# Packed attention with a gated convolution: lower parts of the weights summed on TensorE, some subtractions on VectorE, 1e-9 as a 33rd column

## The chip, the cores and the metric

The kernel runs on one core of one Trainium2 chip, in one launch. The metric is device time in microseconds (us). Before the change three runs took 299.49, 299.0 and 297.74 us: median 299.0 us. Engines: PE is TensorE (PEld its weight loads), DVE is VectorE, ACT is ScalarE, POOL is GpSimd, SP issues all transfers.

## The reference

Eight batches of eight heads, 576 positions, 64 columns per head. A packed set of 32 queries `p` attends over the sequence; the 576 queries `q` then attend over those 32 results; a gated convolution block follows. `w_val`, `conv_w` and `w_out` arrive as 64-bit numbers, all else as 32-bit.

```python
def sm_attn(qq, kk, vv):
    s = scale * np.matmul(qq, kk.transpose(0, 1, 3, 2))
    s = s - np.max(s, axis=-1, keepdims=True)
    a = np.exp(s)
    a = a / (np.sum(a, axis=-1, keepdims=True) + 1e-09)
    return np.matmul(a, vv)
p_packed = sm_attn(p, k, v)
out = sm_attn(q, p_packed, p_packed)
...
for k in range(K):
    gate_pre += conv_w[k][None, None, :] * xp[:, k:k + S, :]
gate = 1.0 / (1.0 + np.exp(-gate_pre))
val = x @ w_val
return (gate * val @ w_out).astype(np.float32)
```

## The kernel before

Every batch is cut into steps, each a Python generator that yields after an instruction or a few. A table, `ORDER`, spells out the sequence in which the steps are advanced; a letter is a step, the digit behind it the batch, and `.n` means n advances. `InOrder` ties each instruction to the one before it on its engine, so the table fixes each engine's queue, and an instruction that waits holds up all that stand behind it there. Between engines only data and buffers make anything wait. The helper has one line (L82), so the profile's rows are told apart by the names of their tiles.

The steps: `P K V Q` load p, k, v, q; `L` loads the weights as pairs of 32-bit words; `W`, `C`, `O` turn `w_val`, `conv_w`, `w_out` into 32-bit form; `k` and `q` transpose on DVE; `a` is the first attention (scores `s<-kT`, the maximum `nb`, the exponential `a<-s`, a transpose `at`/`a1t` on PE and ACT, the product `pv` with v, the normalised `ppd`); `p` turns `ppd` into `ppT`; `s` makes the second scores (`s<-qT`), transposes them on DVE into `t`, takes the maximum `mx`, subtracts on POOL, exponentiates on ACT; `t` sums (`sm`), inverts (`rs`), scales on POOL, transposes back (`a<-t`), and splits the result into a rounded part `a2h` and a remainder `a2l`; `w` multiplies `ppT` by `w_val` (`wp`, split into `wph` and `wpl`); `x` makes the attention output `x` for the gate, in batches 0 to 2 already convolved (`kx`, from `cwb`) and in batches 3 to 7 copied to `xp`; `g` is the gate of batches 3 to 7, four chained multiply-adds per 128 channels on DVE (`sig<-xp,cw,sig`) and a tanh on ACT; `v` multiplies gate and value (`val` on PE, `sig<-sig,val` on DVE) and splits that into `gvh` (a copy on ACT) and `gvl` (a subtraction on POOL); `o` is the projection, twelve matmuls for each 128 output rows from `gvh`, `gvl`, `woh`, `wol`, then a copy `osb` out of PSUM and a store.

`from_double` builds a number from its two words: `top`, from the high word, and `rest`, the low word scaled on ACT, then multiplied on POOL by the power of two of `top`. For `w_val` POOL adds the two (`wv`). For `w_out` ACT rounds half of `top` to `woh`, DVE takes the remainder, and POOL adds `rest` to it (`wol`). The half stands for the 1/2 in sigmoid(z) = (1 + tanh(z/2))/2. The tiles of the weights lie in a pool `stage`, whose space is taken over by `gvh` and `gvl` afterwards; there are two `top` buffers and five of `words`. PSUM has three buffers of two banks (`big`) and two of one bank (`mid`, `out`).

Of the kernel before, what the change touches and what calls it, by code (L numbers as in the profile page):

```python
# [47 lines left out]
ORDER = """
L0 W0 P0 L0 P0 W0.2 k0 K0 W0 k0 K0 W0 L0 W0 V0 K1 W0 k0 a0 W0.2 a0.4 W0 a0.3 W0.3 K1 k1 W0 a0 k1 a0 L0 Q0 W0 k1 L0
a0.2 W0 V0 W0.2 a0 Q0 L0 W0 C0 q0 a1 C0 a1 C0 a0 W0 a1 a0 a1 V1 W0 K2 a1 C0.2 a0 a1 a0 q0 p0.2 O0 C0 a1 s0 C0 O0 a1 s0  # L50
O0 P2 a1 s0.2 L0 s0 O0 s0 O0.2 a1 Q1 a1.2 C0 t0.2 C0 V1 O0.2 C0 s0 W0.3 t0 P2 t0 s0.2 O0 t0 k2 a1 k2 t0.2 W0 C0 O0.2
x0 q1 t0 W0 a1 W0 O0 W0 a1 x0 Q1 a1 w0 O0 a1 q1 O0 t0 O0 p1 O0.2 L0 x0 K2 x0 K3 w0 O0.2 k2 O0 w0 O0 x0 L0 O0 x0 t0
O0.4 a2 O0 x0 v0 O0 k3 V2 p1 O0 a2.2 K3 a2 O0.2 v0 O0 a2 O0 V2 s1 O0.2 s1 a2 O0 | s1 a2.2 s1 v0 a2.2 v0 a2 v0 s1.2 x1
a2 k3 v0.2 t1 v0 t1 v0 s1 a2 w1 a2 w1 P4 a2 v0.2 K4 k3 Q2 t1 s1 v0 a2 w1 a2 v0 P4 p2 t1 V3 v0 s1 v0 t1 a3 t1 V3 v0 t1
a3.2 k4 p2 a3 t1 a3 Q2 t1 a3 o0 a3 x1 k4 a3 q2 t1 a3 x1 o0 x1 q2 a3 x1.2 v1 x1 K4 k4 s2 v1 a3 v1 s2.2 v1 a3 Q3 s2.2 o0
v1 s2 Q3 v1 s2 o0 a3 v1 a4 x2 q3 t2 a3 a4 o0 a4 a3 s2 a3 v1.2 o0 K5 k5 a3 t2 v1 a4.2 s2 t2.2 o0 Q4 a4 p3 t2 P6 o0.2 v1
q3 t2 v1 p3 v1 Q4 v1 a4.2 w2 t2 w2 s3 k5 t2 s3 v1.2 w2 t2 s3.2 t2 V4 s3 o0 K5 o0 x2.2 V4 s3 w3 q4 a4 x2.2 t3 s3 q4 t3
k5 x3 K6 s3 w3 a4 t3 w3 o1 t3.2 a4 s3 t3 x2.2 o1 V5 o1 v2 a4 v2 t3.2 P6 a5 a4 a5 t3 o1 a5 K6 a5.2 v2.2 a4 x3.2 o0 k6
a4 x3 t3 a4.2 x3 a5.2 x3 g3 k6 a5 p4.2 x3 v2 a5 V5 a5.2 k6 a5 g3.2 v2 g3 v2.2 s4 g3 v2 s4.2 o1 g3.2 o1 s4 o1 Q5 g3
s4.2 g3 v2 a5 g3 s4 a5 v2.2 g3 v2 t4 a5 o1 g3 a6 s4 v2 a5 o1.2 t4 g3 q5 o1 a6 g3 t4 w4 Q5 v2 a5 a6 g3 a6 o1 w4 K7 o1  # L60
q5 v2 t4 g3 p5 w4 g3 a6 p5 s4 v3 V6 s5 v3 t4 o1 k7 Q6 t4 v3.2 g3.3 v3 s5 v3 V6 o2 t4 g3 o2 s5 v3 s5 o2 g3 v3.2 t4.2 s5
o2 v3 s5 g3 x4 o1 t4 Q6 v3 o2 v3 x4 o2 x4 v3 x4.2 s5 g3 t5 o2 x4 k7 g4 v3 g4 a6 s5 g4 v3 t5 x4 a6 o2 a6 w5 a6 t5.2 a6
o2 g4 a6 g4 q6 g4 a6 g4 a6 g4 t5 v4 g4 a6 s5 o2.2 a6 g4 w5 t5 g4.2 w5 v4 v3 g4 a6 g4 o3 a6 t5 v4.3 g4 o3 p6 t5 v4.2 p6
v4 g4 o2 v4 g4.3 Q7 q6 v4 o3 g4.4 x5.3 K7 o3 s6 o3.2 v4 V7 t5 o3 s6 x5 v4 x5 o3 k7 s6.2 t5 x5 o3 g5 o3 s6.2 Q7 g5.2 x5
o3 a7 g5 g4 a7 v5 g5 a7 o3 g5 V7 s6 g5 a7.2 o3 v5 s6 a7 g5 v4 a7 o3 s6 v5 a7 o3 t6 w6 a7 v5 w6 g5 v4.2 g5 a7.3 v4 g5
q7 a7 g5 v5 o4 q7 a7 g5 a7 g5 v5 o4 t6 a7 o4 v5 o4 v5 g5 t6 g5 w6 g5 t6.2 a7 p7 o4 t6.2 v5 p7 g5 o4 s7 g5 o4 g5 s7 t6
s7.2 o4 v5 s7.2 o4 g5.3 x6 t6 s7 x6 s7 v5.2 t6 x6 o4 x6.2 v5 o4 g5 t7 v5 x6 g6.3 v5 g6 s7 g6 v5 x6 g6 v6.2 o5 t7 o4 t7
o5 g6 w7 g6 o5.2 t7 g6 o5 t7 g6.2 v6.2 g6 t7 v6 g6 v6 g6.2 o5.2 g6 o5 w7 v6.2 g6 v6 g6 o5.2 w7 g6 v6 g6 t7 g6.3 o5 v6
o5 x7 t7 v6.2 g6 v6 o5 x7 o5 t7 v6.2 o6 x7 o5 x7.2 t7 v7 o6.2 x7 g7.2 o6 g7.3 o6 g7 v7 g7 v7 g7 x7 v7.2 o6 g7 o6.2
g7.3 v7 g7 o6 g7.2 v7.3 g7 o6.2 g7.2 v7 g7 o7 g7 o7 v7.2 g7 v7 g7 o7 g7.2 v7.2 o7 v7 o7.2 o6 o7.13  # L70
# [28 lines left out]
def packed_attention_gated_conv(  # L99
# [329 lines left out]
    def attn_out(b):  # L429
        t2 = st["t2", b] = tile_of("t2", [P, G, NBLK, NP], F32, f"t2_{b}")  # L430
        mx = tile_of("mx2", [P, G, NBLK], F32, f"mx2_{b}")
        s2s = scores(
# [3 lines left out]
        for g in range(G):  # L436
            dve.transpose(
                t2[:, g].rearrange("a y z -> a (y z)").rearrange("a (c i m) -> a c i m", c=2, i=NP),
                in_turn(s2s[g]),
            )  # L440
            yield
            for gs in parts(b):
                if gs.stop != g + 1:
                    continue
                n = gs.stop - gs.start
                t3 = t2[:, gs].rearrange("a g y z -> a (g y) z")
                m3 = mx[:, gs].rearrange("a g y -> a (g y)")
                dve.tensor_reduce(m3, t3, axis=AX.X, op=ALU.max)
                yield
                pool.tensor_tensor(  # L450
                    t3, t3, m3.unsqueeze(2).broadcast_to([P, n * NBLK, NP]), op=ALU.subtract
                )
                yield
                act.activation(t3, t3, AF.Exp, scale=scale)
                yield

    def weighted(b):
        sm = tile_of("sm2", [P, G, NBLK], F32, f"sm2_{b}")
# [4 lines left out]
        for gs in parts(b):  # L463
            n = gs.stop - gs.start
            t3 = st["t2", b][:, gs].rearrange("a g y z -> a (g y) z")
            s3, r3 = (x[:, gs].rearrange("a g y -> a (g y)") for x in (sm, rs))
# [11 lines left out]
            yield
            act.copy(ah[:, gs], a2[:, gs])
            yield  # L480
            (pool if b < 3 else dve).tensor_tensor(al[:, gs], a2[:, gs], ah[:, gs].bitcast(F32), op=ALU.subtract)
# [248 lines left out]
```

## Time and profile before

| | |
|---|---|
| three runs, median | 299.0 us |
| the profiled execution, its own time | 301.0 us |
| its span, first to last instruction | 299.2 us |
| mean granted TensorE clock | 0.945 |
| PE busy | 259.6 us (87%), 3676 matmuls |
| DVE busy | 245.2 us (82%), 349 instructions |
| ACT busy | 164.4 us (55%) |
| POOL busy | 124.6 us (42%) |
| read from HBM, written | 33.57 MB, 9.44 MB |

A row of a grouped view reads: line, engine, operation, output<-input, partitions x elements, count | busy us, mean ns of one | idle time of the engine just before, and what ended it. A row of the timeline or of the chain reads: start, duration, engine, operation, and in brackets the idle time before it and its releaser. In the table by stretches each engine has its busy us, and the last three columns are the granted TensorE clock (1.00 is full speed), the DMA engines' busy share and GB/s.

### The profile page before, as it was taken

How to read it: one execution, taken by the hardware profiler on the slowest of the kernel's cores; microseconds unless marked ns; L12 is line 12 of the kernel's file. 1: busy time of each engine (PE TensorE's matmuls, PEld its weight loads, DVE VectorE, ACT ScalarE, POOL GpSimd, SP SyncE). 2: the span in 40 equal slices, each digit the busy share in tenths (PEclk: the TensorE clock that was granted, in tenths of full speed). 3: DMA queues.
4: the chain of work that ended last, by engine and by line, in shares of the span. 5: the costliest groups of instructions: out<-in, count | busy, mean ns of one | idle time of the engine just before them, and what ended most of it. 6: DMA issues, size and time to landing. Idle time of an engine off the chain costs nothing.

```text
span 299.2 us, 8542 instructions
## 1 busy us (share of the span) xinstructions
PE 259.6 (87%) x3676; PEld 192.0 (64%) x3676; DVE 245.2 (82%) x349; ACT 164.4 (55%) x306; POOL 124.6 (42%) x107
## 2 busy tenths in 40 slices
PE   0465555989999998999999999999999979999984
PEld 0143343457677874768776768867876758778852
DVE  1499569799977898687999999999999989847841
ACT  4155345576753564477573766657764637546412
POOL 1334358659916474314424741541522803511230
PEclk9998555899999999999999999999999979999998
DMA  7999996534952498355467511565010101111004
GB/s 219 303 334 265 271 278 200 149 84 157 290 160 70 142 298 226 95 144 156 139 169 196 184 37 46 184 163 183 37 71 37 38 35 70 62 45 70 35 2 175
DMA packets 25839, 43.56 MB, mean 146 GB/s; under 512 B 5829, under 2 KB 11973, under 8 KB 25802
## 3 DMA queue, kind: packets, MB, share of 16 engines
q1 hardware_dynamic: 25802, 43.02, 48.6%
q8 instruction: 29, 0.48, 0.7%
q14 instruction: 8, 0.07, 0.1%
HBM read 33.57 MB, written 9.44 MB: 144 GB/s over the span
## 4 chain that ended last, share of the span: by engine, by line
PE 56%; DVE 23%; DMA 9%; ACT 5%; issue 3%; SPq 2%; POOL 1%; POOLq 1%; ACTq 0%; DVEq 0%
PE o L82 23%; DVE sig L82 13%; PE val L82 11%; PE x L82 8%; PE s L82 5%; DMA vm<-in_v_dram 3%; PE pv L82 3%; DMA wo_words<-in_moe_w_out_dram 3%; PE at L82 3%; DMA km<-in_k_dram 2%; DVE sm L82 2%; DVE kT L82 2%; SPq L82 2%; PE wp L82 1%; ACT sig L82 1%
## 5 line engine op out<-in xcount | busy, mean ns | idle before, releaser
L82 DVE SCALAR_TENSOR_TENSOR sig<-xp,cw,sig 128x576 f32<-128x576 f32 x80 | 76.5, 957 | 8.7 <-ACT sig L82 7.2
L82 POOL TENSOR_TENSOR gvl<-sig,gvh 128x576 fp32r<-128x576 f32 x32 | 48.4, 1514 | 79.7 <-ACT gvh L82 79.7
L82 PE MATMUL o<-woh,gvh 128*128 128x512 f32 x144 | 59.0, 410 | 2.8 <-ACT osb L82 2.7
L82 PE MATMUL o<-woh,gvl 128*128 128x512 f32 x144 | 57.3, 398 | 1.0 <-POOL gvl L82 1.0
L82 PE MATMUL o<-wol,gvh 128*128 128x512 f32 x144 | 56.9, 395 | 0.0
L82 PE MATMUL val<-a2h,wph 128*128 128x288 f32 x128 | 39.6, 310 | 0.0
L82 PE MATMUL val<-a2h,wpl 128*128 128x288 f32 x128 | 37.8, 295 | 0.0
L82 PE MATMUL val<-a2l,wph 128*128 128x288 f32 x128 | 37.7, 294 | 0.0
L82 ACT COPY osb<-o 128x512 f32<-128x512 f32 x34 | 19.9, 587 | 31.4 <-PE o L82 25.2
L82 PEld LDWEIGHTS o<-woh,gvh 128*128 128x128 f32 x144 | 27.4, 190 | 15.0 <-ACT osb L82 6.3
L82 PEld LDWEIGHTS o<-woh,gvl 128*128 128x128 f32 x144 | 27.3, 190 | 8.3 <-POOL gvl L82 2.1
L82 DVE SCALAR_TENSOR_TENSOR sig<-sig,val 128x576 f32<-128x576 f32 x32 | 23.7, 740 | 9.9 <-PE val L82 5.6
L82 PEld LDWEIGHTS o<-wol,gvh 128*128 128x128 f32 x144 | 27.5, 191 | 4.8
L82 POOL TENSOR_TENSOR t<-t,mx 128x576 f32<-128x576 f32 x16 | 20.8, 1299 | 19.5 <-DVE mx L82 19.4
L82 PE MATMUL pv<-vm,a1t 96*32 96x64 f32 x768 | 16.7, 239 | 13.9 <-ACT a1t L82 8.0
L82 POOL TENSOR_TENSOR t<-t,rs 128x576 f32<-128x576 f32 x16 | 20.6, 1288 | 17.7 <-DVE rs L82 15.0
L82 PEld LDWEIGHTS pv<-vm,a1t 96*32 96x32 f32 x768 | 13.4, 121 | 22.5 <-ACT a1t L82 14.4
L82 PE MATMUL s<-kT,pT 32*32 32x288 f32 x512 | 17.2, 479 | 12.1 <-DVE kT L82 11.7
L82 ACT CAST gvh<-sig 128x576 fp32r<-128x576 f32 x32 | 21.5, 673 | 10.5 <-DVE sig L82 9.4
L82 PEld LDWEIGHTS val<-a2h,wph 128*128 128x128 f32 x128 | 24.1, 188 | 5.0 <-DVE sig L82 1.4
L82 PEld LDWEIGHTS val<-a2h,wpl 128*128 128x128 f32 x128 | 24.1, 188 | 0.4
L82 PEld LDWEIGHTS val<-a2l,wph 128*128 128x128 f32 x128 | 24.1, 188 | 0.0
(81 smaller groups left out, 457.7 us busy)
## 6 DMA issues: line engine op xcount, KB each, us to landing
km<-in_k_dram SPq DMA_DIRECT2D x16, 576.0 KB, 6.1
vm<-in_v_dram SPq DMA_DIRECT2D x16, 576.0 KB, 7.1
qm<-in_q_dram SPq DMA_DIRECT2D x16, 576.0 KB, 5.3
out_dram<-osb SPq DMA_DIRECT2D x36, 256.0 KB, 2.1
wv_words<-in_moe_w_val_dram SPq DMA_DIRECT2D x4, 512.0 KB, 5.9
wo_words<-in_moe_w_out_dram SPq DMA_DIRECT2D x4, 512.0 KB, 10.2
p<-in_p_dram SPq DMA_DIRECT2D x16, 64.0 KB, 3.5
cw_words<-in_moe_conv_w_dram SPq DMA_DIRECT2D x1, 20.0 KB
```

What stands on the lines that cost most here:

```text
L82: made = getattr(self.engine, op)(*args, **kw)
```

## The change

1. `rest` gets a tile of its own (two buffers) in place of the low words. Two constants, `plus` and `minus`, are the identity times 1 and -1. `wv` is now summed by two matmuls (`top` under the identity, `rest` under `plus`) into the `out` bank of PSUM and copied out by ACT. `woh` is `top` rounded, without the half; its remainder is summed by three matmuls (`top`, minus `woh`, plus `rest`) and copied out by ACT. The half is applied where `osb` leaves PSUM.
2. `gvl` of batches 3 to 7 is subtracted on DVE; in batches 0 to 2 on POOL as before.
3. `t` has rows of 33 words; POOL writes 1e-9 into the last of each, and the sum `rs` runs over 33. The addition of `eps` goes. The sums of the first attention get one tile for both halves, so 1e-9 and the reciprocal are one instruction each per batch.
4. The order table is another one. A branch for joined halves (`parts`, not used at `JOINED = 8`) is gone.

```diff
-L0 W0 P0 L0 P0 W0.2 k0 K0 W0 k0 K0 W0 L0 W0 V0 K1 W0 k0 a0 W0.2 a0.4 W0 a0.3 W0.3 K1 k1 W0 a0 k1 a0 L0 Q0 W0 k1 L0
+L0 W0 P0.2 W0.2 K0 W0 L0 K0 W0.2 k0 W0.3 V0 Q0 W0 k0.2 a0 W0 k1 K1 a0 W0.2 a0.2 K1 q0 L0 W0 a0.3 W0 a0 k1 a0 W0.2 L0
...
+    nc.scalar.mul(plus, ident, 1.0)
+    nc.scalar.mul(minus, ident, -1.0)
-    eps = const.tile([P, G * NBLK], F32, name="eps")
-    nc.gpsimd.memset(eps, 1e-9)
...
-            pool.tensor_tensor(rest, rest, hw.bitcast(F32), op=ALU.mult)
...
+        pool.tensor_tensor(rest, low, hw.bitcast(F32), op=ALU.mult)
...
-            pool.tensor_tensor(
-                wv[:, c, :], st["top", f"wv{c}"], words[:, :, 0].bitcast(F32), op=ALU.add
-            )
+            whole = one(f"wv{c}_ps", "out")
+            pe.matmul(whole, ident, st["top", f"wv{c}"], start=True, stop=False)
+            pe.matmul(whole, plus, st["rest", f"wv{c}"], start=False, stop=True)
+            yield
+            act.copy(wv[:, c, :], whole)
...
-            act.mul(hi, top, 0.5)
-            yield
-            dve.scalar_tensor_tensor(
-                top, top, 0.5, hi.bitcast(F32), op0=ALU.mult, op1=ALU.subtract
-            )
-            yield
-            pool.tensor_tensor(lo, top, rest, op=ALU.add)
+            act.copy(hi, top)
+            yield
+            left = one(f"wo{c}_ps", "out")
+            pe.matmul(left, ident, top, start=True, stop=False)
+            pe.matmul(left, minus, hi, start=False, stop=False)
+            pe.matmul(left, plus, rest, start=False, stop=True)
+            yield
+            act.copy(lo, left)
...
-            dve.tensor_scalar_add(rs, rs, 1e-9)
-            dve.reciprocal(rs, rs)
+        dve.tensor_scalar_add(sm, sm, 1e-9)
+        dve.reciprocal(sm, sm)
...
-        t2 = st["t2", b] = tile_of("t2", [P, G, NBLK, NP], F32, f"t2_{b}")
+        t2 = st["t2", b] = tile_of("t2", [P, G, NBLK, NP + 1], F32, f"t2_{b}")
+        pool.memset(t2[:, :, :, NP:], 1e-9)
...
-            dve.tensor_reduce(s3, t3, axis=AX.X, op=ALU.add)
-            dve.tensor_tensor(s3, s3, eps[:, : n * NBLK], op=ALU.add)
-            dve.reciprocal(r3, s3)
+            dve.tensor_reduce(r3, t3, axis=AX.X, op=ALU.add)
+            dve.reciprocal(r3, r3)
...
-            pool.tensor_tensor(
+            (pool if b in ON_POOL["gvl"] else dve).tensor_tensor(
                 lo, gv, hi.bitcast(F32), op=ALU.subtract
             )
...
-                dve.tensor_copy(osb, ops)
+                dve.tensor_scalar(osb, ops, 0.5, None, op0=ALU.mult)
             else:
-                act.copy(osb, ops)
+                act.mul(osb, ops, 0.5)
```

PE's queue ahead of the first convolution (`x_0_0`, `x_0_1` of batch 0), before. `at_1` and `pv_1` belong to the second half of batch 1's first attention, `cwps` and `spread` to the convolution's weights:

```order
L82 MATMUL pv_0_412<-vm_0_326,a1t_0_352 32x64 x24
L82 MATMUL cwps<-ident,cw_top 128x5 x4
L82 MATMUL spread<-cw_top,ident 32x64 x40
L82 MATMUL at_1_527<-ident,a_1_1_331 96x64 x12
L82 MATMUL pv_1_561<-vm_1_467,a1t_1_526 32x64 x24
L82 MATMUL x_0_0_590<-a_0_459,kx_551 64x288 x2
```

The same place after the change:

```order
L83 MATMUL pv_0_423<-vm_0_361,a1t_0_343 32x64 x24
L83 MATMUL at_1_465<-ident,a_1_1_336 96x64 x12
L83 MATMUL cwps<-ident,cw_top 128x5 x4
L83 MATMUL spread<-cw_top,ident 32x64 x40
L83 MATMUL wo_ps<-wo_top,ident 128x512
L83 MATMUL wo_ps<-woh,minus 128x512
L83 MATMUL wo_ps<-wo_rest,plus 128x512
L83 MATMUL pv_1_556<-vm_1_363,a1t_1_464 32x64 x24
L83 MATMUL ppTt_598<-ident,ppd_342 128x128 x3
L83 MATMUL wv_ps<-wv_top,ident 128x512
L83 MATMUL wv_ps<-wv_rest,plus 128x512
L83 MATMUL x_0_0_609<-a_0_484,kx_550 64x288 x2
```

A sum for `w_out` and the last one for `w_val` have come in ahead of the convolution, with batch 1's `ppTt`. Of the other three sums for `w_val` the first is PE's first work, the second stands within batch 0's first attention, the third right ahead of its second scores; the other three for `w_out` come behind the convolution's first half.

DVE's queue in the second softmax of batch 0 (`t`, `mx`, `sm`/`rs`, `a`), before, from the transposition of the second half:

```order
L82 STREAM_TRANSPOSE t_0_366<-s_0_1_369 128x576
L82 TENSOR_SCALAR wo_words<-wo_top 128x512
L82 TENSOR_SCALAR sm_1_1_332<-sm_1_1_332 128x1
L82 RECIPROCAL sm_1_1_332<-sm_1_1_332 128x1
L82 TENSOR_REDUCE sm_0_457<-t_0_366 128x18
L82 TENSOR_TENSOR sm_0_457<-sm_0_457,eps 128x18
L82 RECIPROCAL rs_0_458<-sm_0_457 128x18
L82 COPY cw<-cwps 128x20
L82 SCALAR_TENSOR_TENSOR wo_top<-wo_top,woh 128x512
L82 TENSOR_REDUCE mx_0_367<-t_0_366 128x18
L82 TENSOR_SCALAR wv_words<-wv_words 128x512
L82 STREAM_TRANSPOSE a_0_459<-t_0_366 128x576
```

The same place after:

```order
L83 STREAM_TRANSPOSE t_0_383<-s_0_1_387 128x18x32
L83 TENSOR_REDUCE mx_0_384<-t_0_383 128x18
L83 SCALAR_TENSOR_TENSOR wo_top<-wo_top,wo_words 128x512
L83 TENSOR_REDUCE rs_0_483<-t_0_383 128x18
L83 RECIPROCAL rs_0_483<-rs_0_483 128x18
L83 COPY cw<-cwps 128x20
L83 TENSOR_SCALAR wo_words<-wo_top 128x512
L83 STREAM_TRANSPOSE a_0_484<-t_0_383 128x576
L83 TENSOR_SCALAR wv_words<-wv_words 128x512
L83 TENSOR_REDUCE rs_0_483<-t_0_383 128x18
L83 RECIPROCAL rs_0_483<-rs_0_483 128x18
```

The second maximum now stands right behind its transposition, and the work on `wv_words` behind the first `a<-t`.

DVE's queue at the end, the last two quarters of batch 7's gate and value, before:

```order
L82 SCALAR_TENSOR_TENSOR sig_2_3668<-xp_1_3514,cw,sig_2_3668 128x576 x4
L82 SCALAR_TENSOR_TENSOR sig_2_3668<-sig_2_3668,val_2_3675 128x576
L82 SCALAR_TENSOR_TENSOR sig_3_3707<-xp_1_3514,cw,sig_3_3707 128x576 x4
L82 SCALAR_TENSOR_TENSOR sig_3_3707<-sig_3_3707,val_3_3741 128x576
L82 COPY osb_5_3791<-o_4_3709 128x512
```

And after:

```order
L83 SCALAR_TENSOR_TENSOR sig_2_3661<-xp_1_3494,cw,sig_2_3661 128x576 x4
L83 TENSOR_TENSOR gvl<-sig_1_3608,gvh 128x576
L83 SCALAR_TENSOR_TENSOR sig_2_3661<-sig_2_3661,val_2_3672 128x576
L83 SCALAR_TENSOR_TENSOR sig_3_3686<-xp_1_3494,cw,sig_3_3686 128x576 x3
L83 TENSOR_TENSOR gvl<-sig_2_3661,gvh 128x576
L83 SCALAR_TENSOR_TENSOR sig_3_3686<-xp_1_3494,cw,sig_3_3686 128x576
L83 SCALAR_TENSOR_TENSOR sig_3_3686<-sig_3_3686,val_3_3738 128x576
L83 TENSOR_TENSOR gvl<-sig_3_3686,gvh 128x576
```

The subtraction `gvl` of a quarter stands behind gate work of the next one; on POOL the same rows are gone, and only the softmax's subtractions and scalings are left there for these batches.

More of the change, by code (lines that the diff above doesn't have):

```diff
@@ L32 @@
  'qm': 2,
+ 'rest': 2,
  'sig': 4,
@@ L53 @@
[L53 to L57, printed above, removed]
@@ L164, in packed_attention_gated_conv @@
     make_identity(nc, ident)
+    plus = const.tile([P, P], F32R, name="plus")
+    minus = const.tile([P, P], F32R, name="minus")
+    nc.scalar.mul(plus, ident, 1.0)
+    nc.scalar.mul(minus, ident, -1.0)
     heads = [slice(NP * hl, NP * hl + NP) for hl in range(4)]
-    eps = const.tile([P, G * NBLK], F32, name="eps")
-    nc.gpsimd.memset(eps, 1e-9)
     wv = const.tile([P, NC, DM], F32, name="wv")
@@ L230, in load_weights, with from_double @@
             yield
-    def from_double(nm, words, rows, by=1.0, rest_on_pool=True):
+    def from_double(nm, words, rows):
         top = st["top", nm] = tile_of("top", [P, DM], F32, f"{nm}_top", stage)[:rows]
+        rest = st["rest", nm] = tile_of("rest", [P, DM], F32R, f"{nm}_rest", stage)[:rows]
         hw, lw = words[:, :, 1], words[:, :, 0]
-        bits, rest = top.bitcast(U32), lw.bitcast(F32)
+        bits, low = top.bitcast(U32), lw.bitcast(F32)
         act.mul(top, hw.bitcast(F32), 2.0**-112)
         yield
-        if rest_on_pool:
-            act.mul(rest, lw, 2.0**-52 * by)
-            yield
+        act.mul(low, lw, 2.0**-52)
+        yield
         dve.tensor_scalar(hw, hw, 1 << 31, None, op0=ALU.bitwise_and)
@@ L272, in conv_weights @@
         taps = top
-        dve.tensor_tensor(top, top, words[:, :, 0].bitcast(F32), op=ALU.add)
+        dve.tensor_tensor(top, top, st["rest", "cw"].bitcast(F32), op=ALU.add)
         yield
@@ L436, in attn_out @@
         for g in range(G):
-            dve.transpose(
-                t2[:, g].rearrange("a y z -> a (y z)").rearrange("a (c i m) -> a c i m", c=2, i=NP),
-                in_turn(s2s[g]),
+            t3, m3 = t2[:, g, :, :NP], mx[:, g]
+            dve.transpose(t3, in_turn(s2s[g]))
+            yield
+            dve.tensor_reduce(m3, t3, axis=AX.X, op=ALU.max)
+            yield
+            pool.tensor_tensor(
+                t3, t3, m3.unsqueeze(2).broadcast_to([P, NBLK, NP]), op=ALU.subtract
             )
             yield
[L442 to L449, printed above, removed]
-                pool.tensor_tensor(
[L451 to L455, printed above, removed]
+            act.activation(t3, t3, AF.Exp, scale=scale)
+            yield
     def weighted(b):
-        sm = tile_of("sm2", [P, G, NBLK], F32, f"sm2_{b}")
         rs = tile_of("rs2", [P, G, NBLK], F32, f"rs2_{b}")
@@ L462, in weighted @@
         al = st["al", b] = tile_of("a2l", [P, G, S], F32R, f"a2l_{b}")
[L463 to L466, printed above, removed]
-            dve.tensor_reduce(s3, t3, axis=AX.X, op=ALU.add)
-            dve.tensor_tensor(s3, s3, eps[:, : n * NBLK], op=ALU.add)
-            dve.reciprocal(r3, s3)
+        for g in range(G):
+            t3, r3 = st["t2", b][:, g], rs[:, g]
+            dve.tensor_reduce(r3, t3, axis=AX.X, op=ALU.add)
+            dve.reciprocal(r3, r3)
             yield
+            t3 = t3[:, :, :NP]
             pool.tensor_tensor(
-                t3, t3, r3.unsqueeze(2).broadcast_to([P, n * NBLK, NP]), op=ALU.mult
+                t3, t3, r3.unsqueeze(2).broadcast_to([P, NBLK, NP]), op=ALU.mult
             )
             yield
-            dve.transpose(
-                a2[:, gs].rearrange("a g s -> a (g s)"), t3.rearrange("a y z -> a (y z)")
-            )
[L478 to L481, printed above, removed]
+            dve.transpose(a2[:, g], t3)
+            yield
+            act.copy(ah[:, g], a2[:, g])
+            yield
+            (pool if b in ON_POOL["al"] else dve).tensor_tensor(
+                al[:, g], a2[:, g], ah[:, g].bitcast(F32), op=ALU.subtract
+            )
             yield
@@ L663, in project @@
             if b == B - 1 and c % 2:
-                osb = tile_of("t2", [P, G, NBLK, NP], F32, f"osb_{b}_{c}")
+                osb = tile_of("t2", [P, G, NBLK, NP + 1], F32, f"osb_{b}_{c}")
                 osb = osb.rearrange("a g y z -> a (g y z)")[:, :DM]
```

59 lines of the change are left out of this document (28 added, 31 removed).

## The prediction

> **What bounds the kernel now.** I read the busy times of the page first, then the table of busy time by stretches, then the chain that ended last, and last the waits in the timeline at the places where the chain leaves PE.
>
> ```profile
> PE 259.6 (87%) x3676; PEld 192.0 (64%) x3676; DVE 245.2 (82%) x349; ACT 164.4 (55%) x306; POOL 124.6 (42%) x107
> 0.00:60.00 60.00, 31.82 (x702) 19.18 (x702) 41.18 (x66) 27.94 (x55) 26.23 (x27) 0.77 0.91 252
> 30.00:50.00 20.00, 9.89 (x262) 7.13 (x258) 14.55 (x25) 9.53 (x20) 10.44 (x8) 0.50 0.90 244
> 60.00:80.00 20.00, 18.28 (x379) 13.16 (x380) 19.07 (x32) 13.28 (x26) 16.36 (x13) 1.00 0.58 159
> 80.00:240.00 160.00, 157.98 (x2325) 118.05 (x2323) 144.92 (x206) 96.92 (x184) 68.16 (x57) 1.00 0.45 135
> 140.00:240.00 100.00, 98.84 (x1167) 74.70 (x1165) 97.13 (x134) 61.41 (x109) 42.93 (x36) 1.00 0.38 117
> 240.00:260.00 20.00, 17.93 (x100) 15.06 (x100) 18.22 (x25) 10.24 (x17) 5.67 (x6) 0.91 0.13 52
> 280.00:290.00 10.00, 9.18 (x46) 7.52 (x45) 7.14 (x8) 3.39 (x5) 2.37 (x2) 1.00 0.01 2
> ```
>
> The kernel has two halves. In the first 60 us PE is idle for 28.2, between 30 and 50 us it runs at half clock, and the DMA engines are 91% busy: a start-up made of chains through several engines. From 60 us on PE hardly stops: idle 1.7 us up to 80, 2.0 in the next 160, 2.1 in 240 to 260, 0.8 in 280 to 290. Beside it DVE is 97% busy from 140 to 240. So the change can gain some 7 us at most after 60 us, besides what the lower clock costs there; the rest must come from the start.
>
> **The start.** In the chain:
>
> ```profile
> 30.31 2.51 PE s L82 x63
> 48.43 1.54 POOL kx L82
> 50.02 5.05 PE x L82 x80
> 56.57 2.67 PE x L82 x80
> 107.15 1.02 PE wp L82 x16
> 180.64 2.76 PE o L82 x12
> ```
>
> Batch 0's second scores end at 32.8, its convolution begins at 50.02: 17.2 us for one softmax. In the timeline DVE transposes the second half early and takes its maximum late, behind rows for the weights and behind the first half's sum:
>
> ```profile
> 35.11 0.78 DVE L82 STREAM_TRANSPOSE t<-s 128x576 f32<-128x576 f32 x1
> 39.99 0.74 DVE L82 TENSOR_REDUCE mx<-t 128x18 f32<-128x576 f32 x1
> ```
>
> After the change the maximum follows its transposition, 4.1 us sooner. POOL is then late next. Its queue is two subtractions, a scaling, a weights' product, `kx`, `a2l`, the second scaling: with the groups' means below, and some 1.3 us for the weights' product, 9.5 us, less about 1 where starts overlap, from some 2 us after the scores (a transposition, a maximum), and 0.8 for the last transposition: 12 us in place of 17.2. **Term 1: -5** (bounds -6 and 0).
>
> ```profile
> L82 POOL TENSOR_TENSOR t<-t,mx 128x576 f32<-128x576 f32 x16 | 20.8, 1299 | 19.5 <-DVE mx L82 19.4
> L82 POOL TENSOR_TENSOR t<-t,rs 128x576 f32<-128x576 f32 x16 | 20.6, 1288 | 17.7 <-DVE rs L82 15.0 <-DVE sm L82 2.6
> L82 POOL TENSOR_TENSOR kx<-ppd,cwb 128x640 f32<-128x640 f32 x3 | 4.7, 1564 | 0.0
> L82 POOL TENSOR_TENSOR a2l<-a,a2h 128x576 fp32r<-128x576 f32 x6 | 8.5, 1418 | 7.9 <-ACT a2h L82 7.9
> ```
>
> **The sums on PE.** The rows that go, and the rows next to the new ones:
>
> ```profile
> L82 POOL TENSOR_TENSOR wv<-wv_top,wv_words 128x512 f32<-128x512 f32 x4 | 5.5, 1371 | 0.3
> L82 POOL TENSOR_TENSOR wol<-wo_top,wo_words 128x512 fp32r<-128x512 f32 x4 | 5.2, 1298 | 0.8 <-DVE wo_top L82 0.7
> L82 DVE SCALAR_TENSOR_TENSOR wo_top<-wo_top,woh 128x512 f32<-128x512 f32 x4 | 3.7, 936 | 0.5 <-ACT woh L82 0.3
> L82 PE MATMUL wp<-wv,ppT 64*32 64x512 f32 x128 | 8.7, 601 | 0.0
> L82 ACT COPY osb<-o 128x512 f32<-128x512 f32 x34 | 19.9, 587 | 31.4 <-PE o L82 25.2
> ```
>
> POOL loses 10.7 us, DVE 3.7, ACT gains eight copies of 0.59 (4.7 us, beside 32 us of idle in the first 60). A matmul of the rounded type over 512 columns costs 2.76/12 = 0.23 us. The trace has no full 32-bit product of a whole 128x128 tile: `wp` runs eight products side by side, each in two passes, in 1.02 us. So one costs between 0.46 (two passes of 0.23) and 1.2 (two `wp` records of 0.601); I take 1.0, nearest to `wp`. A sum for `w_val` is then 1.25 us, one for `w_out` 1.5, all eight 11 us at full clock and twice that at half.
>
> By place: the first two for `w_val` and the first for `w_out` fall where PE is idle: nothing; without that cover 2.5 and 3.0 us. The third for `w_val` stands right ahead of the second scores at half clock, 2.5 us, of which the copy of `ppT`, of the kind of `osb`'s 0.59, hides 0.5: +2.0. The fourth waits for POOL's product, which now stands behind the second scaling (about 1.1 us), and takes 2.5, where the transposition took 0.8 anyway: +2.7, with the convolution waiting behind it. **Term 2: +4.7** (0 to 10). The last three for `w_out` come after the convolution, at full clock and between dense work: 4.5 us, against PE's idle 1.7 between 60 and 80 and some of the 2.0 after it. **Term 3: +2** (0 to 4.5).
>
> The convolution's first half took 5.05 us at half clock, the second 2.67 at full:
>
> ```profile
> 54.00:56.00 2.00, 2.00 (x40) 0.35 (x24) 1.72 (x2) 0.84 (x3) 1.92 (x2) 0.77 0.05 16
> 56.00:58.00 2.00, 2.00 (x59) 1.59 (x59) 0.58 (x1) 2.00 (x5) 2.00 (x2) 1.00 0.59 109
> ```
>
> The clock came back about 5 us after PE became dense at 50. With a sum of 2.5 us right ahead of it the wait for the clock starts earlier. **Term 4: -1** (-2.4, the whole difference, to 0). [...]
>
> **The stage that DVE fills.**
>
> ```profile
> L82 POOL TENSOR_TENSOR gvl<-sig,gvh 128x576 fp32r<-128x576 f32 x32 | 48.4, 1514 | 79.7 <-ACT gvh L82 79.7
> L82 DVE TENSOR_TENSOR a2l<-a,a2h 128x576 fp32r<-128x576 f32 x10 | 7.4, 745 | 0.8 <-ACT a2h L82 0.8
> L82 DVE TENSOR_TENSOR sm<-sm,eps 128x18 f32<-128x18 f32 x16 | 6.9, 434 | 0.6
> L82 DVE SCALAR_TENSOR_TENSOR sig<-xp,cw,sig 128x576 f32<-128x576 f32 x80 | 76.5, 957 | 8.7 <-ACT sig L82 7.2
> 194.26 3.37 DVE L82 SCALAR_TENSOR_TENSOR sig<-xp,cw,sig 128x576 f32<-128x576 f32 x4
> 175.54 1.42 POOL L82 TENSOR_TENSOR gvl<-sig,gvh 128x576 fp32r<-128x576 f32 x1 [1.43 <-ACT gvh L82]
> 175.65 1.93 DVE L82 SCALAR_TENSOR_TENSOR sig<-xp,cw,sig 128x576 f32<-128x576 f32 x1
> ```
>
> `a2l` is the same subtraction on DVE: 0.745 us, so twenty `gvl` add 14.9. Against it: the sixteen additions of `eps`, 6.9; the remainders of `w_out`, 3.7; and what POOL costs DVE. A gate row takes 0.843 us alone (3.37/4) but 1.93 beside a `gvl` on POOL, 957 ns in the mean: 80 x 0.114 = 9.1 us lost beside POOL, of which `gvl`, with over half of POOL's time there, may cause 5. Sum for DVE: about -1. But between 140 and 240 us, where three batches' `gvl` fall (12 x 0.745 = 8.9), only seven additions (3.0) and some 2.4 of the loss beside POOL go: +3.5, against 2.9 idle. **Term 5: +0.5** (0 to +3.5).
>
> Rows of `t` become 33 words. The sum over a 33rd column adds 1/32 of 0.735 us, 0.02; eight memsets on POOL cost like the small ones there. [...]
>
> **The two stops at the end.**
>
> ```profile
> 235.50 5.41 DVE L82 SCALAR_TENSOR_TENSOR sig<-xp,cw,sig 128x576 f32<-128x576 f32 x4
> 236.37 1.44 POOL L82 TENSOR_TENSOR gvl<-sig,gvh 128x576 fp32r<-128x576 f32 x1 [1.01 <-ACT gvh L82]
> 241.53 0.57 ACT L82 COPY osb<-o 128x512 f32<-128x512 f32 x1
> 242.16 0.50 PE L82 MATMUL o<-woh,gvh 128*128 128x512 f32 x1 [2.07 <-ACT osb L82]
> 285.87 0.50 PE L82 MATMUL o<-woh,gvl 128*128 128x512 f32 x1 [0.82 <-POOL gvl L82]
> 291.12 0.50 PE L82 MATMUL o<-woh,gvl 128*128 128x512 f32 x1 [0.18 <-POOL gvl L82]
> ```
>
> At 235.5 four gate rows took 5.41 us, not 3.37, beside POOL; the tanh behind them, on ACT the `osb` copy behind the tanh, and PE behind the copy: 2.07 us, and a granted clock of 0.91 over 20 us (1.8 us). With that `gvl` off POOL the delay of 2.04 us halves at least, and the order there is another. **Term 6: -3.4** (-3.9 to 0). At the end PE waits twice for `gvl`, 1.0 us; on DVE it takes 0.745 in place of 1.5, and the gate rows ahead of it run alone. The new wait: a `gvl` waits for its copy on ACT (of the kind of `osb`'s 0.59), and the next quarter's gate stands behind it on DVE; two to four gate rows (1.7 us and more) are put in between, except for the last, behind which only two output copies stand. **Term 7: -1** (-2 to 0).
>
> **Sum:** -5 + 4.7 + 2 - 1 + 0.5 - 3.4 - 1 = -3.2 us. The profiled execution took 301.0 us (span 299.2), 2.0 above the median of the three runs, so it would become 297.8, and the median 299.0 - 3.2 = **295.8**.
>
> **Rivals.**
> - *DVE becomes the bound between 140 and 240.* Its 97% busy, 3.5 us more, speaks for it; that it has 12 us idle between 80 and 140 (160 - 144.92, less the 2.9) against. Term 5 at +3.5: 298.8.
> - *Slower: the sums hold up PE's queue.* PE takes its queue in order; a sum needs ACT, three DVE rows and a POOL row first, and runs at half clock. If the first three early sums aren't hidden either, term 2 rises from 4.7 by 5.5 to about 10: 301.3. The point from which it decides: a convolution that begins after 53 us.
> [...]
> - *The sums are hidden altogether.* Terms 2 and 3 at 2.5 together: 291.6. For it: PE's 28 us idle; against: half clock and the chain behind them.
> - *Nothing is done that the names say*, the order alone counting: the listing shows the instructions gone, so I give it nothing.
>
> **Chances.** Forecast (293.5 to 298) 0.48, DVE 0.16, PE's queue 0.16, rows 0.07, hidden 0.13. A measurement of this kernel tells about 0.5% from no change, 297.5 to 300.5 here. Faster: nearly all of the first, the last: 0.60. Same: DVE, rows: 0.22. Slower: 0.18. The range leaves out a tenth on each side: 290.0 to 301.5.
>
> **What would show it.** The convolution of batch 0 beginning near 49.7 us and the clock at 1.00 soon after (terms 1, 2, 4); PE idle below 2 us between 60 and 80 with twelve `wo_ps` records there or before; gate rows near 0.87 us in the mean; no PE wait over 1 us for `osb` or `gvl` after 230. I am wrong if the convolution begins after 53, if DVE has no idle time and PE over 4 us of it between 140 and 240, or if `t`'s passes take over 0.80 us.

## The result, and the profile after

Twenty runs of the changed kernel beside twenty of the one before give medians of 296.17 and 299.49 us: the ratio is **0.9898, 95% interval [0.9873, 0.9924]**, about 3 us faster. Medians here are over all runs, while each ratio leaves out the executions that the chip ran in a slower state, so the two need not agree to the last digit. Its profiled execution took 297.13 us (span 295.3, mean clock 0.977); that of before took 301.0.

The busy times on the page of the changed kernel:

```profile
PE 269.6 (91%) x3704; PEld 194.2 (66%) x3704; DVE 238.9 (81%) x333; ACT 168.0 (57%) x316; POOL 82.6 (28%) x86
```

Its table of busy time by stretches, the stretches as before, and three short ones around the start of the convolution:

```profile
0.00:60.00 60.00, 41.22 (x783) 22.08 (x784) 39.86 (x59) 32.88 (x66) 20.59 (x24) 0.89 0.86 250
60.00:80.00 20.00, 19.92 (x399) 14.89 (x406) 18.98 (x29) 15.06 (x30) 12.43 (x10) 1.00 0.57 159
80.00:240.00 160.00, 157.70 (x2254) 116.94 (x2239) 141.74 (x197) 95.81 (x182) 47.90 (x50) 1.00 0.46 136
140.00:240.00 100.00, 99.70 (x1159) 74.21 (x1158) 96.05 (x135) 62.65 (x112) 21.12 (x24) 1.00 0.31 93
240.00:260.00 20.00, 19.98 (x137) 14.94 (x137) 17.91 (x25) 11.98 (x21) 1.72 (x3) 1.00 0.14 53
46.00:48.00 2.00, 1.70 (x5) 1.03 (x5) 2.00 (x3) 1.49 (x4) 1.58 (x2) 0.50 0.20 71
48.00:50.00 2.00, 2.00 (x19) 0.81 (x25) 1.90 (x4) 1.10 (x2) 0.30 (x1) 0.51 0.01 4
50.00:52.00 2.00, 2.00 (x80) 1.18 (x64) 2.00 (x3) 0.00 (x0) 0.42 (x1) 1.00 0.06 12
```

PE is 10 us busier and still ends earlier: POOL's 124.6 us became 82.6, and the hole between 240 and 260 is gone (19.98 busy at full clock, before 17.93 at 0.91). Between 140 and 240 DVE is as full as before (96.05) and PE idles 0.3 us, not 1.2.

The chain that ended last, at the start, at the first value product of batch 1, and at the end:

```profile
32.40 1.77 PE s L83 x62
...
46.30 0.90 PE ppTt L83 x3
47.20 2.13 PE wv_ps L83 x3
49.34 2.89 PE x L83 x80
...
53.24 1.52 PE wo_ps L83 x4
...
86.44 1.79 PE val L83 x12
...
272.10 8.43 PE o L83 x36
...
287.79 0.60 ACT osb L83
```

From the second scores' end (34.17) to the end of the convolution's first half (52.23) it takes 18.1 us; before, from 32.82 to 55.07, 22.2. I use this **start stretch** below, since it hangs less on when the loads came in. PE runs without a break from `ppTt` into the sum and the convolution. Between the scores and `ppTt` the chain also names a load of q, which ends at 45.85; in the second profile, below, it names none there, and the same rows stand at the same distances, so the load is not taken for the cause.

The groups that the forecast spoke of:

```profile
L83 DVE SCALAR_TENSOR_TENSOR sig<-xp,cw,sig 128x576 f32<-128x576 f32 x80 | 66.7, 834 | 1.3 <-ACT sig L83 0.5
L83 DVE TENSOR_TENSOR gvl<-sig,gvh 128x576 fp32r<-128x576 f32 x20 | 15.0, 749 | 3.3 <-ACT gvh L83 3.3
L83 DVE TENSOR_REDUCE rs<-t 128x18 f32<-128x594 f32 x16 | 12.3, 766 | 1.1 <-ACT t L83 1.1
L83 DVE STREAM_TRANSPOSE t<-s 128x576 f32<-128x576 f32 x16 | 12.3, 769 | 4.8 <-PE s L83 4.8
```

A gate row fell from 957 to 834 ns, which pays 9.8 us of the 15.0 that `gvl` adds to DVE.

### The profile page after: what moved, and what is told of

Same layout as the page of the kernel before. It is cut to its first block, busy times and chain, and to the rows that moved or that the text cites. A ratio compares the mean times of both kernels' runs of the same rounds, so it can differ in the third digit from the quotient of the medians.

```text
span 295.3 us, 8555 instructions
## 1 busy us (share of the span) xinstructions
PE 269.6 (91%) x3704; PEld 194.2 (66%) x3704; DVE 238.9 (81%) x333; ACT 168.0 (57%) x316; POOL 82.6 (28%) x86
## 4 chain that ended last, share of the span: by engine, by line
PE 69%; DVE 14%; DMA 6%; issue 5%; ACT 3%; SPq 1%; DVEq 0%; ACTq 0%
PE o L83 27%; PE val L83 14%; DVE sig L83 7%; PE x L83 7%; PE s L83 6%; PE pv L83 4%; DMA qm<-in_q_dram 4%; PE at L83 3%; DMA km<-in_k_dram 3%; PE wp L83 2%; PE wv_ps L83 2%; PE wo_ps L83 1%; DVE gvl L83 1%; SPq L83 1%; PE ppTt L83 1%
## 5 line engine op out<-in xcount | busy, mean ns | idle before, releaser
L83 DVE SCALAR_TENSOR_TENSOR sig<-xp,cw,sig 128x576 f32<-128x576 f32 x80 | 66.7, 834 | 1.3 <-ACT sig L83 0.5
L83 ACT ACTIVATE osb<-o 128x512 f32<-128x512 f32 x34 | 20.3, 596 | 29.9 <-issue 14.4
L83 DVE STREAM_TRANSPOSE kT<-km 128x1152 f32<-128x1152 f32 x16 | 21.7, 1359 | 4.0 <-DMA km<-in_k_dram 4.0
L83 POOL TENSOR_TENSOR gvl<-sig,gvh 128x576 fp32r<-128x576 f32 x12 | 17.1, 1429 | 24.2 <-ACT gvh L83 24.2
L83 ACT ACTIVATE sig<-sig 128x576 f32<-128x576 f32 x20 | 13.7, 687 | 15.5 <-DVE sig L83 15.4
L83 DVE STREAM_TRANSPOSE qT<-qm 128x1152 f32<-128x1152 f32 x16 | 21.6, 1352 | 0.0
```

Source lines behind the costliest of these rows:

```text
L83: made = getattr(self.engine, op)(*args, **kw)
```

## The experiments

Each run stands against runs of the kernel before on the same chip. "The changed kernel" has the ratio 0.9898 above, 0.9876 in the first run below; differences are taken to both, in us of 299.

**The changed kernel again.** No edit.

> The changed kernel as it is, profiled a second time and beside its own variants. In its first profile the projection's twelve matmuls took 2.81 and 3.00 us in place of 2.76 and 2.95 before. Theory A: that belongs to the kernel (where its tiles lie); then they take 2.80 us and more again. Theory B: it belongs to the chip or that one execution; then they take 2.76 again and the time is some 2 us lower (294 us). Time otherwise 296 us, 1.0% below before.

294.59 us, ratio 0.9876 [0.9835, 0.9917]. The chunks took 2.81 and 3.00 us again, so their length belongs to the kernel (Theory A); that the time is the 294 us of Theory B comes from elsewhere. The chain at the start:

```profile
30.47 1.51 PE s L83 x62
...
38.63 2.86 PE wo_ps L83 x4
...
44.24 0.90 PE ppTt L83 x3
45.14 2.08 PE wv_ps L83 x3
47.22 2.60 PE x L83 x80
```

The second scores took 1.51 us here, against 1.77 in the first profile, where the clock was 0.64 from 30 to 34, and the start stretch took 17.8 us (31.98 to 49.82). The convolution begins at 47.2 here and at 49.3 in the first profile: that place alone moves by 2 us from one execution to the next. The first sum for `w_out` ends at 41.5, before `ppTt`.

**`gvl` on POOL again.**

```diff
-ON_POOL = {'al': (0, 1, 2), 'gvl': (0, 1, 2)}
+ON_POOL = {'al': (0, 1, 2), 'gvl': (0, 1, 2, 3, 4, 5, 6, 7)}
```

> The changed kernel with all 32 gvl on POOL again, its order kept. Theory A (terms 5 to 7: gvl on POOL makes the gate rows beside it slow, delays the gate, and the last gvl come late): POOL 112 us, gate rows 0.93 us in the mean, waits of PE for gvl of 0.2 to 0.8 us at the end, DVE about 2 us less busy, the time 1 to 4 us above the changed kernel. Theory B (the new order alone took the stops away): within 0.7 us of it, no PE wait over 1 us behind 230 us.

299.93 us, ratio 1.0057 [1.0024, 1.0089]: 4.8 to 5.4 us above the changed kernel, more than Theory A's upper end. The waits for `gvl` that Theory A expected at the end did not come; behind 225 us PE waits 1.6 us in all for `osb`. Its stretches:

```profile
140.00:240.00 100.00, 97.75 (x1151) 73.17 (x1151) 95.46 (x121) 60.89 (x108) 41.21 (x36) 1.00 0.31 93
240.00:260.00 20.00, 19.75 (x134) 14.50 (x133) 18.81 (x23) 12.26 (x20) 6.12 (x6) 1.00 0.15 54
```

and DVE in its timeline near the end:

```profile
261.72 3.38 DVE L83 SCALAR_TENSOR_TENSOR sig<-xp,cw,sig 128x576 f32<-128x576 f32 x4 [1.78 <-ACT sig L83]
...
266.53 4.62 DVE L83 SCALAR_TENSOR_TENSOR sig<-xp,cw,sig 128x576 f32<-128x576 f32 x4
```

The stop at 240 stays away with `gvl` on POOL, as it does in the new order with the sums put back (PE busy 19.95 of these 20 us) or with 1e-9 added (19.98): the new order does without that stop, whichever of these edits is undone. But with `gvl` on POOL a gate row takes 971 ns in the mean, not 834: of the two rows above one has four of them in 3.38 us, the other in 4.62, of which the chain gives a single one 2.07 (at 267.38). PE loses 2.0 us more between 140 and 240 and ends late.

**`gvl` on DVE, in the order of before.**

```diff
-            pool.tensor_tensor(
+            (pool if b < 3 else dve).tensor_tensor(
                 lo, gv, hi.bitcast(F32), op=ALU.subtract
```

> The kernel before, in its own order, with nothing changed but gvl of batches 3 to 7 on DVE. Theory A (terms 5 to 7 are the work of that subtraction alone): the stop at 240 and the waits for gvl at the end go, the time is 3 to 5 us below before (294 to 296). Theory B (it pays only with the order made for it, since DVE is full between 140 and 240): PE idles 2 us more there, the time within 1 us of before or above it.

306.45 us, ratio 1.0241 [1.0186, 1.0295]: 7 us slower than before. Its stretches:

```profile
140.00:240.00 100.00, 94.25 (x1117) 69.47 (x1116) 96.42 (x137) 59.06 (x104) 22.74 (x22) 1.00 0.38 112
240.00:260.00 20.00, 17.86 (x100) 14.01 (x100) 17.65 (x26) 9.73 (x16) 2.54 (x4) 0.91 0.14 52
```

and the new group on DVE:

```profile
L82 DVE TENSOR_TENSOR gvl<-sig,gvh 128x576 fp32r<-128x576 f32 x20 | 15.9, 795 | 4.7 <-ACT gvh L82 4.6
```

and two of PE's waits (us in total, times, the longest one):

```profile
PE o L82 <- DVE gvl L82: 2.8, 2, 2.1
PE o L82 <- ACT osb L82: 0.7, 1, 0.7
```

Theory B: PE idles 5.8 us between 140 and 240 (before 1.2) beside a full DVE, and DVE itself stands 4.6 us before `gvl` waiting for the copy on ACT (3.3 in the changed kernel). Between 240 and 260 there is a stop as long as before, but it is another one. The wait for `osb` is down from 2.1 us to 0.7; instead PE waits 2.1 us for `gvl` itself (246.36 to 247.12 in the chain), which stands on DVE behind four gate rows (241.88 to 245.60). So the old stop goes with either, `gvl` off POOL or the new order; in the old order the move puts a new one in its place. The same move costs 7 us in one order and saves 5 in the other (the two kernels differ in the weights' sums as well).

**The weights' sums back on POOL and DVE, all of them; only `w_val`'s; only `w_out`'s.** In the second and third run one of the two pieces stands alone.

```diff
-            whole = one(f"wv{c}_ps", "out")
-            pe.matmul(whole, ident, st["top", f"wv{c}"], start=True, stop=False)
-            pe.matmul(whole, plus, st["rest", f"wv{c}"], start=False, stop=True)
-            yield
-            act.copy(wv[:, c, :], whole)
+            pool.tensor_tensor(wv[:, c, :], st["top", f"wv{c}"], st["rest", f"wv{c}"].bitcast(F32), op=ALU.add)
+            yield
...
-            left = one(f"wo{c}_ps", "out")
-            pe.matmul(left, ident, top, start=True, stop=False)
-            pe.matmul(left, minus, hi, start=False, stop=False)
-            pe.matmul(left, plus, rest, start=False, stop=True)
+            dve.tensor_tensor(top, top, hi.bitcast(F32), op=ALU.subtract)
             yield
-            act.copy(lo, left)
+            pool.tensor_tensor(lo, top, rest.bitcast(F32), op=ALU.add)
```

> The changed kernel with the weights' lower parts added on POOL and DVE again as before (the half and the new order stay). Theory A (terms 2 to 4 as forecast: sums on PE cost 4.7 and 2 and gave 1 by the clock): PE about 12 us less busy, the time 2 to 5 us lower, the convolution of batch 0 begins at 46 to 48 us. Theory B (the sums pay: POOL's additions stood in the chain ahead of the convolution, and PE's sums woke the clock): the convolution begins after 50 us, its first half takes 4 us and more, the time is 0 to 3 us higher.

> The changed kernel with only the four sums for w_val back on POOL. Theory A (term 2 as forecast: they cost PE 4.7 us on the path, less what the clock gave): convolution at 46 to 48 us, time 1 to 3 us below the changed kernel. Theory B (with them POOL's queue sets the start, as where all eight were put back: 50.6): convolution after 50 us, its first half 4 us or more, time 2 to 4 us above.

> The changed kernel with only the four sums for w_out back on DVE and POOL. Theory A (term 3 as forecast: the sums cost PE 2 us): time 1 to 2 us below the changed kernel, PE idle under 1 us between 60 and 80. Theory B (DVE's four remainders, 3.7 us, stand ahead of rows that PE waits for): PE idle 2 to 4 us between 60 and 80 and the time 1 to 4 us above.

| sums back | time, us | ratio | start stretch, us |
|---|---|---|---|
| none (changed kernel) | 294.59 | 0.9876 [0.9835, 0.9917] | 17.8 |
| `w_val` | 294.01 | 0.9828 [0.9776, 0.988] | 16.9 (18.3 in the last run below) |
| `w_out` | 300.88 | 1.0047 [1.0012, 1.0083] | 22.2 |
| both | 300.29 | 1.0041 [1.0017, 1.0065] | 22.2 |

The start stretch is read from one execution each. With all sums on PE it took 17.8 and 18.1 us in the two profiles of the changed kernel and 17.3, 17.9 and 19.2 in three runs of this document whose start is the same or nearly so (the unused tiles, 1e-9 added, `gvl` on POOL). So 16.9 or 18.3 is not told apart from these; 22.2, twice, is.

The two halves of one edit go opposite ways. `w_val`'s sums on PE cost 1.4 to 2.1 us by the ratios, if anything (Theory A; the intervals overlap, and beside `w_out`'s they make no difference, 1.0041 against 1.0047). `w_out`'s save 4.5 to 5.1 (Theory B, for one reason more than it named). With `w_out`'s back the whole gain of the start stretch is gone. ACT's timeline of the run with `w_out`'s back:

```profile
45.39 0.32 ACT L83 ACTIVATE ppd<-pv,sm 128x64 f32<-128x64 f32 x1 [1.11 <-PE pv L83]
50.03 0.66 ACT L83 ACTIVATE wo_top<-wo_words 128x512 f32<-128x512 f32 x1 [4.33 <-POOL wol L83]
50.60 0.35 ACT L83 ACTIVATE ppd<-pv,sm 128x128 f32<-128x128 f32 x1
```

PE's longest wait of that run (us in total, times, the longest one):

```profile
PE ppTt L83 <- ACT ppd L83: 5.7, 1, 5.7
```

its stretch behind the start:

```profile
60.00:80.00 20.00, 15.75 (x374) 10.79 (x365) 19.41 (x27) 10.99 (x23) 13.18 (x12) 1.00 0.70 189
```

and POOL in its timeline:

```profile
45.73 1.60 POOL L83 TENSOR_TENSOR t<-t,rs 128x576 f32<-128x576 f32 x1
...
48.74 1.26 POOL L83 TENSOR_TENSOR wol<-wo_top,wo_rest 128x512 fp32r<-128x512 f32 x1
```

There are two `top` buffers. ACT wants to write the next `wo_top`, and waits 4.33 us until POOL's `wol` has read the old one; `wol` stands in POOL's queue behind the whole softmax and a product for `w_val`. Behind ACT's wait stands the second part of `ppd`, behind that `ppTt`, and PE idles 5.7 us. In the second profile of the changed kernel the sum on PE ended 9.5 us after the second scores (41.5 and 31.98, above); `wol` here ends 15.3 us after them (50.0; the scores at 34.7). After 60 us PE then idles 4.3 us (before 1.7, changed kernel 0.1) beside a full DVE.

**`w_out`'s sums on PE in the order of before**, with `gvl` on DVE as in the run above. The new code of `w_out` is put into that kernel, with the half applied at `osb`.

> The kernel before, in its own order, with gvl of batches 3 to 7 on DVE and the four sums for w_out on PE (half at osb, as in the changed kernel); w_val's sums stay on POOL. Against the same without the sums. Theory A (the sums for w_out pay by themselves, since they take four DVE rows and four POOL rows from between 45 and 80 us): 2 to 5 us lower than that. Theory B (term 3: they cost PE 2 us, and paid only because the new order has room): 0 to 3 us higher.

308.18 us, ratio 1.0302 [1.0252, 1.0352]: by the ratios 1.8 us above the same without the sums (the intervals overlap), and surely not 2 us below it: Theory B. Of its stretches:

```profile
60.00:80.00 20.00, 18.47 (x360) 13.19 (x362) 14.43 (x25) 13.35 (x28) 11.21 (x10) 1.00 0.43 127
```

Between 60 and 80 DVE drops from 19.1 to 14.4 us and PE waits as before: in that order DVE's rows for the weights were not what PE waited for.

**The second maximum late.** Only the order table changes: in batch 0 the first half's sum and scaling come ahead of the second maximum.

```diff
-a1 s0 K2 O0.2 s0.2 a1 O0 s0.2 O0 s0 a1.2 C0 t0.2 C0 O0 W0 O0.2 C0 s0 C0 K2 W0.2 O0 a1 t0 x0 t0.2 V2 a1 W0 t0.2 W0.2 t0
+a1 s0 K2 O0.2 s0.2 a1 O0 s0 O0 a1.2 C0 t0.2 s0.2 C0 O0 W0 O0.2 C0 s0 C0 K2 W0.2 O0 a1 t0 x0 t0.2 V2 a1 W0 t0.2 W0.2 t0
```

> The changed kernel with the second maximum of batch 0 behind the first half's sum and scaling again, as before; the order is otherwise kept. Theory A (term 1: that maximum sets the start, worth 5 us): convolution after 51 us, the time 3 to 6 us above the changed kernel. Theory B (PE's own queue, with the fourth sum for w_val last, begins the convolution): it begins within 1 us of the changed kernel's 47 to 49, and the time is within 1 us.

297.95 us, ratio 0.9956 [0.9926, 0.9986]: 1.7 to 2.4 us above the changed kernel, between the theories. Its profile is of an execution of 302.68 us, the longest of the twelve, so only the start stretch is read: 20.6 us against 17.3 to 19.2 in the five profiles above. Part of that is the clock: the convolution's first half, at half clock until 56.3 us, took 4.25 us, against 2.89 and 2.60 in the two profiles of the changed kernel.

**The fourth sum for `w_val` behind the convolution's first half.**

```diff
-W0 O0 a1 O0 a1 O0.3 p1 W0 x0 Q1 P2 L0 k2 t0 q1 O0 k2 q1 K3 W0 x0 w0 O0.2 x0 O0 w0 x0 k2 O0.3 K3 w0 x0 t0 O0 a2 O0 x1
+W0 O0 a1 O0 a1 O0.3 p1 x0 W0 Q1 P2 L0 k2 t0 q1 O0 k2 q1 K3 W0 x0 O0.2 x0 O0 w0.2 x0 k2 O0.3 K3 w0 x0 t0 O0 a2 O0 x1
```

> The changed kernel with the fourth sum for w_val behind the first half of the convolution in place of ahead of it, and wp behind the next sum for w_out. Theory A (the clock comes back a time after PE became dense, whatever it does): the convolution begins 2 us sooner relative to the transposition ppTt ahead of it and takes about 2 us longer, 4 to 5 us; with a short wait for the sum's copy the time is 0 to 1 us above the changed kernel. Theory B (the sum is a plain 2.1 us on the path, as term 2 has it): the first half stays near 2.9 us and the time is 1 to 2 us lower. Theory C (it is the full-size product that wakes the clock): the first half takes 5 us and the time is 2 us higher.

298.85 us, ratio 0.9954 [0.9906, 1.0001]. From its chain:

```profile
44.84 0.90 PE ppTt L83 x3
45.74 4.30 PE x L83 x80
50.04 1.30 PE wv_ps L83 x3
...
52.01 1.85 PE wo_ps L83 x4
53.86 1.10 PE wp L83 x16
```

The convolution takes the sum's place behind `ppTt`, and its half takes 4.30 us, not 2.89: Theory A's picture. From `ppTt`'s end to the second half's start it is 9.1 us (45.74 to 54.80) against 7.5 (47.20 to 54.69). Of the 2.1 us of the sum ahead, the shorter convolution gave back 1.4; the sum itself takes 1.3 us in its later place, and a wait of 0.7 for its copy comes behind it. The time rose 1.7 to 2.3 us, as Theory C had it, but its mechanism is out: the clock is back at 48.5 us, within the convolution, and the next full-size product comes at 50.04. The rise is more than the 1.6 of this place; its interval does not tell the rest apart. That a sum ahead is no rule for the clock is shown in the last section.

**1e-9 added on DVE, 32 words a row.**

```diff
-        pool.memset(t2[:, :, :, NP:], 1e-9)
...
             dve.tensor_reduce(r3, t3, axis=AX.X, op=ALU.add)
+            dve.tensor_tensor(r3, r3, eps, op=ALU.add)
```

> The changed kernel with rows of 32 words in t, no memset, and 1e-9 added on DVE in an instruction of its own again (sixteen of 0.3 to 0.43 us). Theory A (33-word rows cost nothing, and what DVE saves is hidden): DVE 5 to 7 us busier, t passes 0.74 and 0.77 us as in the changed kernel, the time 0 to 1.5 us higher. Theory B (33-word rows cost more than they save, or shift what stands behind them in memory and slow PE): the time 1 to 3 us lower.

295.56 us, ratio 0.9918 [0.9876, 0.9961]: not told apart from the changed kernel; DVE is 2.4 us busier, not 5 to 7. Its sum row took 746 ns, that over 33 words 766; the transpositions into `t` took 769 both times. The sixteen additions came to 4.3 us of DVE (269 ns each).

**Two unused tiles.** Nothing is computed with them; they only move what lies behind.

```diff
+    const.tile([P, 40], F32, name="pad0")
+    sb.tile([P, 40], F32, name="pad1")
     wv = const.tile([P, NC, DM], F32, name="wv")
```

> The changed kernel with two unused tiles of 160 bytes per partition, so that woh, wol, gvh and gvl stand as in the kernel before, to a multiple of 1024 bytes (woh: 26400 for 26240, before 25376). Theory A (the longer projection comes from where its operands lie): twelve matmuls of a chunk take 2.76 us again in place of 2.81 and 2.95 in place of 3.00, in all about 1.8 us less (293 us). Theory B (something else, or another tile): 2.81 and the time of the changed kernel.

294.39 us, ratio 0.9846 [0.9796, 0.9897]. The chain at the end, to be read against the changed kernel's 8.43 for the same 36 matmuls:

```profile
263.59 1.59 PE val L83 x12
265.18 2.76 PE o L83 x12
...
269.52 8.20 PE o L83 x36
```

Theory A: 0.228 us for a projection matmul in place of 0.234, by addresses alone. A chunk of 12 took 2.76 us, not 2.81; over 36 chunks that is 1.8 us. The time fell by 0.9 to 1.6, with an interval as wide as that.

**Both gains together**: `w_val`'s sums on POOL, and the two unused tiles.

> The changed kernel with the four sums for w_val back on POOL and the two unused tiles of 160 bytes, both together. Theory A (the two gains lie apart and add up): the projection's chunks take 2.76 and 2.95 us, the time is 1.5 to 2 us below that with the sums alone (294.0): 292 to 293, 2.0 to 2.5% below before. Theory B (beside PE's shorter chunks DVE, 97 us busy of 100 between 140 and 240, becomes the bound): the chunks are shorter, but PE idles over 1 us more in that stretch and the time stays at 294.

**292.75 us, ratio 0.9793 [0.9746, 0.984]**: faster than the kernel before, and by the median than the changed one (the interval lies below that of its first measurement and just touches that of the second). The chunks took 2.76 us, and PE idled 0.7 us between 140 and 240: Theory A, though the step from 294.0 is 1.2 us, not 1.8.

## Why the prediction was right, step by step

The forecast was 295.8 us from a sum of -3.2; the median is 296.2, the span fell by 3.9. What it named to look for is there: convolution at 49.27 (49.7 forecast; 47.15 in the second profile, so this match is partly luck), clock 1.00 from 50 us, PE idle 0.1 us between 60 and 80, gate rows 834 ns, no wait above 0.7 us at the end. The sum came out better than its terms. Up to the first value product of batch 1 the terms said +0.7 us and the profile shows -1.7; from there on they said -3.9 and it shows -2.2. That the two misses nearly cancel is luck.

- **The start (terms 1, 2 and 4).** For the start stretch they said 22.2 - 5 + 2.7 - 1 = 18.9 us; it took 17.8 to 18.1. The picture, the sum right ahead of the convolution and PE's queue setting its begin, held. The working of term 1 adds up to 11.3 us, not 12 (9.5 - 1 + 2 + 0.8). The reason given for it was part of it: with the maximum late again the time rises by 1.7 to 2.4 us (the stretch, in one profile, by 1.4 to 3.3), not by 5. It needs the first `w_out` sum on PE as well, which the prediction booked as "nothing", because it falls where PE is idle. That sum frees a `top` buffer; without it all 4.1 us go, with the maximum still early. This wait of ACT for a buffer is the step that the prediction did not have.
- **Term 2** (+4.7) was too dear: putting `w_val`'s sums back gains 1.4 to 2.1 us, if anything. The place and length were right (2.13 us at half clock); the convolution first, without a sum ahead, took 1.4 us longer in its one profile, so there the sum gave that much back. **Term 4** was mis-sized: 2.89 us against 5.05, so -2.2 where -1 was taken. The comparison with the convolution first accounts for 1.4 of it. The rest is open, because the same code gives 2.6 to 4.0 us for this half from one profile to the next.
- **Term 3** (+2) holds as PE work: three sums of 1.3 to 1.5 us, 4.4 us, against 1.6 us of idle time that went. In the order of before the sums cost about 1.8 us, if anything. In the new one they pay 4.5 to 5.1, so as a price of the sums its sign was wrong: the term counted PE alone and not who had waited for DVE's remainders and for the buffer.
- **Term 5** (+0.5): the loss did not come; PE idles 0.3 us where it idled 1.2. DVE's sum was mis-sized: it became 6.3 us less busy, not 1, since the gate rows fell by 9.8 us where 5 was taken. Its rival, DVE as the bound, is what happens in the old one: PE idles 4.6 us more, which the rival put at 3.5.
- **Terms 6 and 7** (-4.4) were right in size: the two stops that went are 2.07 us, 1.8 by the clock (0.91 over 20 us) and 1.0, together 4.9. Their reason was half of it. `gvl` off POOL does take the wait for `osb` away, but in the old order PE then waits as long for `gvl` on DVE, and in the new order the stop stays away with `gvl` on POOL too. What the move saves in the new order, 4.8 to 5.4 us, therefore lies elsewhere: 2.0 us of it between 140 and 240.
- **33 words:** the forecast's sum has no term for them, and the rows that the chances give 0.07 did not turn dear: DVE's two transpositions of the softmax took 769 ns each and its maximum 740, with 33 words and with 32. DVE's sum took the 0.02 us more (766 and 746 ns).
- **Not foreseen:** 1.8 us for where the projection's operands lie.

At the first value product of batch 1 the changed kernel leads by 1.7 us: it begins at 86.44, and before, in the chain, it was

```profile
85.46 0.81 PE pv L82 x48
...
88.97 1.79 PE val L82 x12
```

with that `pv` already done, which comes later in the new order. From there on the lead grew by 2.2 us: 4.9 from the two stops and 0.9 between 140 and 240, less 1.8 for the longer chunks and 1.1 of new idle time between 80 and 140 (60 less 157.70 - 99.70, against 60 less 157.98 - 98.84). The last 0.7 us of this account stay open, and it is one profile against one: in the second profile of the changed kernel that product begins at 84.00. Open too is which places of the new table carry its worth: no run has it alone, without the other edits.

## What to carry to other kernels

Moving work to an idle engine was worth what it freed: a buffer released 9.5 us behind the second scores, not 15.3, was worth more than the work itself, and the profile shows it as a wait of the engine that writes the buffer next (4.33 us on ACT). An edit and a fixed order are one change: `gvl` on DVE cost 7 us in the old table and saved 5 in the new, so try each edit with its order, and the parts of an edit apart, because one half can pay for the other. After any new tile, compare a repeated matmul's pitch: here addresses alone moved it by 2 to 3% (2.81 to 2.76 us for twelve, 8.43 to 8.20 for 36). And a stretch read from one profile can move by 2 us with the same code (the convolution began at 49.3 and at 47.2), so take several before a difference of that size is called a cause.
